# Operand sums of the 512-to-2048 weights on GpSimd, and three pairs of the last matrix formed early, kept in DRAM and read back

## The chip, the cores and the metric

The kernel runs on one core of one Trainium2 chip. The metric is device time in microseconds of one execution. An execution is called a run; the time before is the median of three runs.

## The reference, cut to what matters

```
out_g, out_l = attention with 32 global positions and a band of +-32 around each local one
x = concat([out_g, out_l]) as (2176, 512)
h = max(x @ w1, x @ w2, x @ w3)          # 512 -> 768
y = h @ w_out                            # 768 -> 512
g = softplus(y @ w_in)                   # 512 -> 2048
return g @ w2_out                        # 2048 -> 512
```

All arrays come in as float64. The kernel takes the words apart itself and computes with float32 halves: an operand is a high part plus a low part, and a product is three matmuls (high by high, high by low, low by high).

## The kernel before, in words

There are four stages. The first is the attention. The second, 512 to 768 to 512, works on eight units of tokens, 0 to 7 (256 tokens where the number is even, 288 where it is odd); `up` multiplies a unit by one of the three up weights (12 matmuls, 18 `up`s for a unit), `down` and `down_all` multiply by `w_out`. The third, 512 to 2048, and the fourth, 2048 to 512, use Strassen's scheme: seven products of half-size blocks in place of eight, so that operands are first summed and differenced. The names PE, DVE, ACT, POOL and SP stand for TensorE, VectorE, ScalarE, GpSimd and the queue that issues the DMAs. The order on every engine is the order in which the code is written out; generators (`d4`, `d5`, `vgen`, `vloads`, `words`, `load_x`, `load_o`) are advanced a step at a time between pieces of the main work, at rates such as `WU`, `WD`, `VD`, `VL`, `VE`.

Names that the steps need:

- `split(w, src)` makes the two halves of an operand: ACT copies the high part (L644), POOL subtracts it from the source (L645).
- `dec_w4` forms the seven operands of one of eight pairs of blocks of `w_in`: it reads a pair `qi` from DRAM, sums it (L671, L672, L678, L686, four instructions of 256 columns) and splits it. Pairs 0 to 3 (`d4`) are formed beside units 6 and 7, pairs 4 to 7 (`d5`) beside the first half of the third stage.
- `load_o(t)` does the same to the tokens of one quarter: sums on DVE (L709, L712, L717, L725, 544 columns each), seven splits on ACT and POOL. It runs one quarter ahead of the products that use it; its split of `x[1]` is the first that `prods_b` of the next quarter reads.
- The third stage is 32 steps i. In step i, PE does `prods_a(i)` (3 products, 18 matmuls of 272 columns), `prods_c(i-1)` (2), `prods_b(i)` (2). ACT copies the first product to `e` (L964), DVE adds it to the second (L965), and only then may `prods_b` add on to that second product: its matmuls at L943 wait for L965. DVE's L973, L974, L986 and L987 form the other sums.
- `make_v` (the generator `vgen`) forms the operands of the last matrix, eight pairs p: it reads `vq`, sums it (L1020 with 512 columns, L1022, L1023, L1025 with 256) and splits it. It starts at step 16; pairs 4 and 5 go to a place that is free from step 28, pairs 6 and 7 are formed beside the first products of the fourth stage.
- The fourth stage is a list of items (block of tokens, pair). For each item DVE does three sums (L1085 to L1087) and two low parts (L1093), ACT two high parts (L1092), PE 21 matmuls of 256 columns (L1097 to L1099).
- `load_x(u)` reads a unit's tokens `xr` from DRAM, ACT and DVE split them (L113, L114). The tokens of units 6 and 7 are both loaded at the end of unit 5, one behind the other.
- All DMAs are issued by SP, in order: an issue that waits holds back those behind it.
- Pools that matter: `wp`, 24 buffers for weights and operands, `cp`, 8 more from unit 6 on, and `raw`, 3 buffers. `room` and `free4` count how many `w_in` operands may be placed.

Of the kernel before, what the change touches and what calls it, by code (L numbers as in the profile page):

```python
# [8 lines left out]
F32 = mybir.dt.float32  # L9
# [3 lines left out]
ALU = mybir.AluOpType  # L13
# [8 lines left out]
def body(ctx, tc, kq, vw, vb, qg, w1, w2, w3, w_out, w2_in, w2_out, out):  # L22
# [475 lines left out]
    od = [dram.tile([128, 4, 544], F32, name=f"od{i}") for i in range(4)]  # L498
    gd = [dram.tile([128, 4, 2176], F32, name=f"gd{i}") for i in range(4)]
# [69 lines left out]
    def down_all(u):  # L569
# [3 lines left out]
        for f in range(6):  # L573
            w = W[3, f]
# [72 lines left out]
    n4, free4 = [0], [0]  # L647

# [7 lines left out]
    def dec_w4(ps, tile_q):  # L656
        half = None
# [9 lines left out]
        for p in ps:  # L667
# [3 lines left out]
            nc.vector.tensor_tensor(s[:, 0], a21, a22, op=ALU.add)  # L671
            nc.vector.tensor_tensor(s[:, 1], s[:, 0], a11, op=ALU.subtract)  # L672
# [26 lines left out]
            wi[p] = [wa[:, 0], wa[:, 1], h, wb[:, 0], wb[:, 1], wc[:, 1], wc[:, 0]]  # L699

# [32 lines left out]
    with tc.manual_schedule():  # L733
# [116 lines left out]
        for u in range(6):  # L850
# [4 lines left out]
            loads_x = [] if u == 0 else [6, 7] if u == 5 else [u + 1]  # L855
# [32 lines left out]
        d4 = dec_w4(range(4), lambda: dp.tile([128, 4, 256], F32, tag="raw", name="qi", bufs=3))  # L888
# [292 lines left out]
        for i in range(32):  # L1181
# [29 lines left out]
        vgate[0] = 2  # L1211
# [82 lines left out]
```

## Time and profile before

| | us |
|---|---|
| median of 3 runs | 808.92 (807.06 to 809.92) |
| the profiled execution | 808.67 |
| its span, first to last instruction | 807.0 |
| PE busy | 761.6 (94%) |
| DVE busy | 601.6 (75%) |
| ACT busy | 362.3 (45%) |
| POOL busy | 231.4 (29%) |
| granted TensorE clock, mean | 0.989 of 2.4 GHz |

The profiled execution lies 1.7 us above its span. A busy time is a sum over instructions that are queued one behind the other; PE's matmuls overlap, so PE can be busy all the time and still be slow, which the count of matmuls in a stretch shows better. The third stage runs from 433.7 to 617.7 us, the fourth from there to the end; units 6 and 7 are PE's work from 356.4 to 433.7 us.

### The profile page before, as it was taken

The page shows a single profiled execution, that of the slowest core. Times are in us where ns is not written, and L with a number is a line of the kernel's source. Part 1 is how long each engine was busy: PE and PEld are TensorE (multiplying, and loading weights), DVE is VectorE, ACT ScalarE, POOL GpSimd, SP SyncE. Part 2 cuts the span into 40 slices and gives each one's busy share as a digit, 9 for nine tenths or more (in the row PEclk, how much of TensorE's full clock was granted, in tenths as well). Part 3 has the DMA queues.
Part 4 walks back from the last instruction along what each step waited for, and adds up shares of the span by engine and source line. Part 5 has one row for each costly group of instructions (what it writes and reads, how often), then busy time and mean ns, then how long its engine had stood idle before and what let it go on. Part 6 is the DMA issues. An engine that isn't in the chain of part 4 may idle for free.

```text
span 807.0 us, 18054 instructions
## 1 busy us (share of the span) xinstructions
PE 761.6 (94%) x6984; PEld 728.7 (90%) x6984; DVE 601.6 (75%) x1486; ACT 362.3 (45%) x935; POOL 231.4 (29%) x212
## 2 busy tenths in 40 slices
PE   5789998999999999999999989999988889999998
PEld 3579997999989889999999989999888789999998
DVE  5978965988976967328922778557767989999996
ACT  6865446545544523024312445435435444444443
POOL 4545431222111200006800766315654330000000
PEclk9999999999999999999999999999999999999999
DMA  8858028777776636123003544345536803444432
GB/s 334 341 185 299 37 90 275 231 268 253 260 263 215 202 124 208 28 74 132 15 1 124 192 137 144 120 164 181 189 123 214 262 2 105 131 132 132 131 93 79
DMA packets 76134, 130.94 MB, mean 162 GB/s; under 512 B 9616, under 2 KB 45328, under 8 KB 76048
## 3 DMA queue, kind: packets, MB, share of 16 engines
q1 hardware_dynamic: 76048, 129.79, 47.5%
q8 instruction: 55, 0.90, 0.5%
q14 instruction: 31, 0.25, 0.1%
HBM read 91.29 MB, written 38.47 MB: 161 GB/s over the span
## 4 chain that ended last, share of the span: by engine, by line
PE 76%; DVE 12%; issue 3%; ACT 3%; DMA 3%; POOL 2%; SPq 0%; POOLq 0%; ACTq 0%; DVEq 0%
PE pu L513 8%; PE pu L514 8%; PE pu L515 8%; PE z L1098 6%; PE z L1099 6%; PE z L1097 6%; PE z L943 6%; PE z L945 6%; PE z L944 6%; PE pd L560 2%; PE pd L561 2%; PE pd L559 2%; DMA raw<-in_w_dram 2%; PE pog L294 2%; PE ps L142 2%
## 5 line engine op out<-in xcount | busy, mean ns | idle before, releaser
L513 PE MATMUL pu<-xh,w 128*128 128x256 f32 (+1 forms) x576 | 169.4, 294 | 1.5 <-ACT xo L255 1.0
L515 PE MATMUL pu<-xh,w 128*128 128x256 f32 (+1 forms) x576 | 166.9, 290 | 0.8 <-POOL w L451 0.8
L514 PE MATMUL pu<-xl,w 128*128 128x256 f32 (+1 forms) x576 | 167.4, 291 | 0.2
L943 PE MATMUL z<-o,wi 128*128 128x272 f32 x448 | 131.7, 294 | 11.4 <-DVE h L965 10.1
L1099 PE MATMUL z<-v,oo 128*128 128x256 f32 x480 | 137.1, 286 | 4.0 <-DVE oo L1093 4.0
L1098 PE MATMUL z<-v,oo 128*128 128x256 f32 x480 | 136.7, 285 | 1.3 <-POOL v L645 1.3
L1097 PE MATMUL z<-v,oo 128*128 128x256 f32 x480 | 135.9, 283 | 1.7 <-ACT oo L1092 0.9
L945 PE MATMUL z<-o,wi 128*128 128x272 f32 x448 | 131.3, 293 | 0.0
L944 PE MATMUL z<-o,wi 128*128 128x272 f32 x448 | 130.7, 292 | 0.0
L513 PEld LDWEIGHTS pu<-xh,w 128*128 128x128 f32 x576 | 109.3, 190 | 4.8 <-ACT xo L255 1.2
L515 PEld LDWEIGHTS pu<-xh,w 128*128 128x128 f32 x576 | 109.0, 189 | 1.2 <-POOL w L451 1.2
L514 PEld LDWEIGHTS pu<-xl,w 128*128 128x128 f32 x576 | 109.2, 190 | 0.8 <-DVE xl L114 0.6
L943 PEld LDWEIGHTS z<-o,wi 128*128 128x128 f32 x448 | 86.6, 193 | 13.1 <-DVE h L965 11.2
L1099 PEld LDWEIGHTS z<-v,oo 128*128 128x128 f32 x480 | 91.6, 191 | 5.6 <-DVE oo L1093 5.6
L1097 PEld LDWEIGHTS z<-v,oo 128*128 128x128 f32 x480 | 92.1, 192 | 2.5 <-ACT oo L1092 1.6
L1092 ACT ACTIVATE oo<-sm 128x640 fp32r<-128x640 f32 (+1 forms) x72 | 49.8, 692 | 98.2 <-DVE sm L1087 92.3
L1098 PEld LDWEIGHTS z<-v,oo 128*128 128x128 f32 x480 | 91.5, 191 | 1.7 <-POOL v L645 1.7
L945 PEld LDWEIGHTS z<-o,wi 128*128 128x128 f32 x448 | 86.4, 193 | 0.0
L944 PEld LDWEIGHTS z<-o,wi 128*128 128x128 f32 x448 | 86.3, 193 | 0.0
L164 POOL TENSOR_TENSOR s<-s,rs 128x512 f32<-128x512 f32 x32 | 36.2, 1132 | 157.7 <-DVE rs L162 85.5
L645 POOL TENSOR_TENSOR o<-ot,o 128x544 fp32r<-128x544 f32 x36 | 51.2, 1434 | 68.4 <-DVE h L986 38.9
L996 ACT ACTIVATE a<-h 128x816 f32<-128x816 f32 x32 | 28.4, 887 | 92.7 <-DVE h L974 92.7
(145 smaller groups left out, 1665.1 us busy)
## 6 DMA issues: line engine op xcount, KB each, us to landing
gd<-a SPq DMA_DIRECT2D x32, 544.0 KB, 3.1
gl<-gd SPq DMA_DIRECT2D x32, 512.0 KB, 5.6
kq<-in_kq_dram SPq DMA_DIRECT2D x31, 448.0 KB, 5.6
raw<-in_w_out_dram SPq DMA_DIRECT2D x22, 512.0 KB, 4.6
raw<-in_w_dram SPq DMA_DIRECT2D x18, 512.0 KB, 7.9
vt<-in_vw_dram SPq DMA_DIRECT2D x16, 512.0 KB, 6.3
raw<-in_w_in_dram SPq DMA_DIRECT2D x16, 512.0 KB, 4.6
ot<-od SPq DMA_DIRECT2D x24, 272.0 KB, 3.7
```

Of the source, the lines that this page charges most:

```text
L164: nc.gpsimd.tensor_tensor(s[:, :, 0:128], s[:, :, 0:128], rs.unsqueeze(2).to_broadcast([128, 4, 128]), op=ALU.mult)
L513: nc.tensor.matmul(p, lhsT=w[:, 0, k], rhs=xh[:, k, 0:n], start=(k == 0), stop=False)
L514: nc.tensor.matmul(p, lhsT=w[:, 0, k], rhs=xl[:, k, 0:n], start=False, stop=False)
L515: nc.tensor.matmul(p, lhsT=w[:, 1, k], rhs=xh[:, k, 0:n], start=False, stop=(k == 3))
L645: nc.gpsimd.tensor_tensor(w[:, 1], src, w[:, 0].bitcast(F32), op=ALU.subtract)
L943: nc.tensor.matmul(z, lhsT=w[:, 0, k], rhs=x[:, 0, k], start=st and k == 0, stop=False, skip_group_check=True)
L944: nc.tensor.matmul(z, lhsT=w[:, 0, k], rhs=x[:, 1, k], start=False, stop=False, skip_group_check=True)
L945: nc.tensor.matmul(z, lhsT=w[:, 1, k], rhs=x[:, 0, k], start=False, stop=sp and k == 1, skip_group_check=True)
L1092: nc.scalar.activation(oh[:, a:b], src, AF.Copy)
L1097: nc.tensor.matmul(p, lhsT=oh[:, a], rhs=w[:, 0], start=st, stop=False, skip_group_check=True)
L1098: nc.tensor.matmul(p, lhsT=oh[:, a], rhs=w[:, 1], start=False, stop=False, skip_group_check=True)
L1099: nc.tensor.matmul(p, lhsT=ol[:, a], rhs=w[:, 0], start=False, stop=sp, skip_group_check=True)
```

## The change

- Unit 5's loop now loads unit 6's tokens between its own `up`s; only unit 7's remain for its end.
- `dec_w4` takes the engine of its sums as an argument: VectorE for pairs 0 to 3, as before, GpSimd for pairs 4 to 7.
- A new generator, `spill_v`, follows pairs 0 to 3 in `d4`, beside units 6 and 7: it forms pairs 5, 6 and 7 of the last matrix (sums on DVE, splits on ACT and POOL) and writes the halves to DRAM (`vd`). `WU` and `WD`, the steps of `d4` per `up` and per step of `down_all`, go from 0.9 and 1.0 to 1.1 and 1.2, and `d4` is now drained before the third stage.
- `make_v` forms only pairs 0 to 4. The sums of pairs 0 to 2 are on GpSimd, those of 3 and 4 on VectorE; each pair's sums are advanced in turns with the splits of the pair before. It starts at step 14 at a steady rate of 2.2 steps.
- `vload` reads pairs 5 to 7 back with four DMAs each, one DMA in each of the steps 29 to 31, one after them, and one for each of the first items.

```
+    vd = {p: dram.tile([128, 7, 2, 256], F32, name=f"vd{p}") for p in range(5, 8)}
...
-            nc.vector.tensor_tensor(s[:, 0], a21, a22, op=ALU.add)
-            nc.vector.tensor_tensor(s[:, 1], s[:, 0], a11, op=ALU.subtract)
+            eng.tensor_tensor(s[:, 0], a21, a22, op=ALU.add)
+            eng.tensor_tensor(s[:, 1], s[:, 0], a11, op=ALU.subtract)
...
+    def sum_v(eng, q, s):
+        eng.tensor_tensor(s[:, 0:2], q[:, 0:4:2], q[:, 1:4:2], op=ALU.add)
+        yield
+        eng.tensor_tensor(s[:, 2], q[:, 0], q[:, 3], op=ALU.add)
+        eng.tensor_tensor(s[:, 3], q[:, 1], q[:, 3], op=ALU.subtract)
+        yield
+        eng.tensor_tensor(q[:, 2], q[:, 2], q[:, 0], op=ALU.subtract)
+        yield
+
+    def spill_v(ps):
...
+        for p in ps:
+            q, s = [dp.tile([128, 4, 256], F32, tag="raw", name="qv", bufs=3) for _ in range(2)]
+            read_v(q, p)
...
+            for _ in sum_v(nc.vector, q, s):
+                yield
+            for n, y in enumerate((q[:, 0:4:3], s[:, 0:2], s[:, 2:4])):
...
+                w = w4tile()
+                split(w.rearrange("p a t n -> p t a n"), y)
+                write(vd[p][:, 2 * n:2 * n + 2], w)
+                yield
...
-        WU = 0.9
-        WD = 1.0
+        WU = 1.1
+        WD = 1.2
...
+                if u == 5 and i == 2:
+                    if f == 0:
+                        ensure(6)
+                        x6 = load_x(6)
+                    next(x6, None)
-            loads_x = [] if u == 0 else [6, 7] if u == 5 else [u + 1]
+            loads_x = [] if u == 0 else [7] if u == 5 else [u + 1]
...
+        d4 = itertools.chain(d4, spill_v(range(5, 8)))
...
-        d5 = dec_w4(range(4, 8), lambda: wp.tile([128, 4, 256], F32, tag="w", name="qi"))
-        need4(3)
+        d5 = dec_w4(range(4, 8), lambda: wp.tile([128, 4, 256], F32, tag="w", name="qi"), nc.gpsimd)
+        for _ in d4:
+            pass
...
+            for p in range(5):
+                while p == 4 and not vgate[0]:
                     yield
+                nx = iter(())
+                if p < 4:
+                    vs[p + 1] = wp.tile([128, 4, 256], F32, tag="w", name="vs")
+                    nx = sum_v(nc.vector if p > 1 else nc.gpsimd, vq[p + 1], vs[p + 1])
                 for _ in vsplit(p):
                     yield
+                    if next(nx, 1) is None:
+                        yield
...
+            if i > 28:
+                next(vloads)
```

Three places show what moves. The first is DVE in the third stage, step 5 to step 6 (`h`, `e` and `z` are the product sums, `ot` the tokens being summed, `qi` and `s` the `w_in` pair). Before:

```order
L987 TENSOR_TENSOR h<-h,z 128x272
L712 TENSOR_TENSOR ot<-ot 128x544
L671 TENSOR_TENSOR s<-qi 128x256
L672 TENSOR_TENSOR s<-s,qi 128x256
L678 TENSOR_TENSOR qi<-qi 128x256
L965 TENSOR_TENSOR h<-e,z 128x272
```

The same place on DVE now, where L762, L767, L1020, L1028, L1029 and L1042 are what L712, L717, L965, L973, L974 and L987 were:

```order
L1042 TENSOR_TENSOR h<-h,z 128x272
L762 TENSOR_TENSOR ot<-ot 128x544
L1020 TENSOR_TENSOR h<-e,z 128x272
L1028 TENSOR_TENSOR h<-e,z 128x272
L1029 TENSOR_TENSOR h<-h,z 128x272
L767 TENSOR_TENSOR ot<-ot,t_6547 128x544
```

The three sums of `qi` and `s` that stood between the two sums of `h` are gone from DVE.

The second is POOL over steps 5 to 7, where the tokens of quarter 2 (`o_6472` before, `o_6543` now) and a `w_in` pair are split in turns. Before:

```order
L645 TENSOR_TENSOR o_6472<-ot,o_6472 128x544
L645 TENSOR_TENSOR o_6472<-t_6476,o_6472 128x544
L645 TENSOR_TENSOR o_6472<-ot,o_6472 128x544
L645 TENSOR_TENSOR wi<-qi,wi 128x2x256
L645 TENSOR_TENSOR wi<-qi,wi 128x256
L645 TENSOR_TENSOR o_6472<-ot,o_6472 128x544 x2
L645 TENSOR_TENSOR wi<-s,wi 128x2x256
L645 TENSOR_TENSOR o_6472<-ot,o_6472 128x544 x2
```

The same place on POOL now:

```order
L647 TENSOR_TENSOR o_6543<-ot,o_6543 128x544
L647 TENSOR_TENSOR o_6543<-t_6547,o_6543 128x544
L647 TENSOR_TENSOR o_6543<-ot,o_6543 128x544
L673 TENSOR_TENSOR s<-qi 128x256
L674 TENSOR_TENSOR s<-s,qi 128x256
L647 TENSOR_TENSOR wi<-qi,wi 128x2x256
L680 TENSOR_TENSOR qi<-qi 128x256
L647 TENSOR_TENSOR wi<-qi,wi 128x256
L647 TENSOR_TENSOR o_6543<-ot,o_6543 128x544 x2
L688 TENSOR_TENSOR qi<-qi,s 128x256
L647 TENSOR_TENSOR wi<-s,wi 128x2x256
L647 TENSOR_TENSOR o_6543<-ot,o_6543 128x544 x2
```

Four sums of 256 columns now stand ahead of the last two splits of the quarter's tokens, which are `x[1]` and `x[6]`.

The third is DVE beside units 6 and 7, from the last sum of pair 3 on (`m` is the running maximum over the three up products `pu`, `hh` and `hl` its halves). Before:

```order
L686 TENSOR_TENSOR qi<-qi,s 128x256
L527 TENSOR_TENSOR m<-m,pu 128x256 x2
L544 CAST hh<-m 128x256
L545 TENSOR_TENSOR hl<-m,hh 128x256
L527 TENSOR_TENSOR m<-m,pu 128x288 x2
L527 TENSOR_TENSOR m<-m,pu 128x256
```

The same place on DVE now:

```order
L688 TENSOR_TENSOR qi<-qi,s 128x256
L528 TENSOR_TENSOR m<-m,pu 128x288
L767 TENSOR_TENSOR ot<-ot,t_5349 128x544
L528 TENSOR_TENSOR m<-m,pu 128x288
L528 TENSOR_TENSOR m<-m,pu 128x256
L707 TENSOR_TENSOR qv<-qv 128x512
L709 TENSOR_TENSOR qv<-qv 128x256
L710 TENSOR_TENSOR qv<-qv 128x256
L528 TENSOR_TENSOR m<-m,pu 128x256
L545 CAST hh<-m 128x256
L546 TENSOR_TENSOR hl<-m,hh 128x256
L712 TENSOR_TENSOR qv<-qv 128x256
```

The last sum of pair 3 comes three `up`s earlier, and the four sums of each spilled pair (L707, L709, L710, L712) follow between the maxima.

## Rows read from the trace of the kernel before

**Rows 1.** Busy time by stretch: start:end, us, each engine's busy us (instructions), PEclk, DMA share, GB/s.

```profile
361.00:367.40 6.40, 5.88 (x25) 5.04 (x26) 3.40 (x8) 3.50 (x7) 0.00 (x0) 0.74 0.95 303
433.70:498.00 64.30, 58.74 (x451) 58.08 (x452) 46.01 (x74) 29.10 (x59) 37.55 (x28) 0.97 0.47 158
498.00:560.00 62.00, 62.00 (x497) 62.00 (x497) 39.45 (x76) 27.85 (x56) 23.04 (x19) 1.00 0.45 161
560.00:621.70 61.70, 56.28 (x421) 55.50 (x420) 44.24 (x79) 29.91 (x60) 35.96 (x28) 0.94 0.52 177
621.70:667.00 45.30, 38.33 (x280) 35.49 (x279) 40.96 (x84) 20.21 (x40) 17.27 (x11) 0.96 0.39 125
667.00:803.00 136.00, 136.00 (x1138) 136.00 (x1137) 124.61 (x327) 60.15 (x125) 0.00 (x0) 1.00 0.36 115
```

**Rows 2.** PE's waits from 355 us: line, released by: us in total, times, longest.

```profile
PE z L943 <- DVE h L965: 10.1, 5, 2.8
PE z L1099 <- DVE oo L1093: 4.0, 8, 2.0
```

**Rows 3.** Timeline of DVE, steps 5 and 6: start us, us, engine, line, operation.

```profile
466.55 1.65 DVE L712 TENSOR_TENSOR ot<-ot 128x544 f32<-128x544 f32 x1
468.12 1.58 DVE L671 TENSOR_TENSOR s<-qi 128x256 f32<-128x256 f32 x1
469.73 1.45 DVE L672 TENSOR_TENSOR s<-s,qi 128x256 f32<-128x256 f32 x1
471.11 1.48 DVE L678 TENSOR_TENSOR qi<-qi 128x256 f32<-128x256 f32 x1
472.51 0.42 DVE L965 TENSOR_TENSOR h<-e,z 128x272 f32<-128x272 f32 x1
```

**Rows 4.** Timeline of DVE, sums of the last matrix with POOL idle.

```profile
612.25 0.68 DVE L1020 TENSOR_TENSOR vs<-vq 128x512 f32<-128x512 f32 x1
612.85 0.42 DVE L1022 TENSOR_TENSOR vs<-vq 128x256 f32<-128x256 f32 x1
```

**Rows 5.** Timeline of DVE, the same sums beside POOL's work, step 23.

```profile
562.32 0.98 DVE L1020 TENSOR_TENSOR vs<-vq 128x512 f32<-128x512 f32 x1
563.22 0.95 DVE L1022 TENSOR_TENSOR vs<-vq 128x256 f32<-128x256 f32 x1
564.10 1.58 DVE L1023 TENSOR_TENSOR vs<-vq 128x256 f32<-128x256 f32 x1
565.60 1.55 DVE L1025 TENSOR_TENSOR vq<-vq 128x256 f32<-128x256 f32 x1
```

**Rows 6.** POOL by line and shape, 510 to 550 us: busy us, mean ns, idle before.

```profile
L645 POOL TENSOR_TENSOR v<-vs,v 128x512 fp32r<-128x512 f32 x2 | 2.5, 1294 | 4.0 <-PE z L945 4.0
L645 POOL TENSOR_TENSOR v<-vq,v 128x256 fp32r<-128x256 f32 x1 | 0.7, 742 | 2.5 <-ACT v L644 2.5
```

**Rows 7.** Timeline of POOL, steps 6 and 7, in brackets the idle time before.

```profile
475.17 2.85 POOL L645 TENSOR_TENSOR o<-ot,o 128x544 fp32r<-128x544 f32 x2 [2.00 <-ACT o L644]
481.30 2.69 POOL L645 TENSOR_TENSOR o<-ot,o 128x544 fp32r<-128x544 f32 x2 [2.02 <-ACT o L644]
```

**Rows 8.** Timeline of PE, the first matmul of `prods_b(8)`.

```profile
484.35 0.29 PE L943 MATMUL z<-o,wi 128*128 128x272 f32 x1
```

**Rows 9.** Busy time by stretch, beside units 6 and 7; columns as in rows 1.

```profile
368.00:403.00 35.00, 35.00 (x281) 35.00 (x280) 32.87 (x44) 14.79 (x31) 29.23 (x22) 1.00 0.11 38
403.00:434.00 31.00, 30.09 (x237) 29.63 (x236) 6.14 (x14) 6.35 (x17) 1.36 (x1) 1.00 0.07 23
```

**Rows 10.** Timeline of DVE and of PE at the start of the fourth stage.

```profile
622.16 1.88 DVE L1093 TENSOR_TENSOR oo<-sm,oo 128x640 fp32r<-128x640 f32 x1
...
624.10 0.39 PE L1099 MATMUL z<-v,oo 128*128 128x256 f32 x1 [1.97 <-DVE oo L1093]
```

**Rows 11.** Timeline of PE, the first matmul of unit 7.

```profile
361.25 0.40 PE L513 MATMUL pu<-xh,w 128*128 128x288 f32 x1 [0.44 <-ACT xh L113]
```

**Rows 12.** DMA issues: out<-in, queue, operation, count, KB each, median us to landing.

```profile
gl<-gd SPq DMA_DIRECT2D x32, 512.0 KB, 5.6
```

More of the change, by code (lines that the diff above doesn't have):

```diff
@@ L573, in down_all @@
         for f in range(6):
+            need((3, f))
             w = W[3, f]
@@ L647, in body @@
     n4, free4 = [0], [0]
+    halves = {}
     def w4tile():
@@ L654, in room, with dec_w4 @@
         return n4[0] + n <= NC + free4[0]
-    def dec_w4(ps, tile_q):
-        half = None
+    def dec_w4(ps, tile_q, eng):
         qs = {}
@@ L699, in dec_w4, with read_v, write @@
             wi[p] = [wa[:, 0], wa[:, 1], h, wb[:, 0], wb[:, 1], wc[:, 1], wc[:, 0]]
+    def read_v(q, p):
+        nc.sync.dma_start(out=q.rearrange("p a n -> p (a n)"), in_=qd["v"][p].rearrange("p a n -> p (a n)"))
+    def sum_v(eng, q, s):
[7 more added lines that the diff above has]
+    def spill_v(ps):
+        half, out = None, []
+        def write(d, w):
+            out.append((d, w))
+            if len(out) > 1:
+                x = out.pop(0)
+                nc.sync.dma_start(out=x[0], in_=x[1].bitcast(F32))
+                if x[1].shape[1] == 2 and len(x[1].shape) == 4:
+                    free4[0] += 1
+        for p in ps:
[6 more added lines that the diff above has]
+            for n, y in enumerate((q[:, 0:4:3], s[:, 0:2], s[:, 2:4])):
+                while not room(1):
+                    yield
+                w = w4tile()
+                split(w.rearrange("p a t n -> p t a n"), y)
+                write(vd[p][:, 2 * n:2 * n + 2], w)
+                yield
+            if p % 2 == 0 or half is None:
+                while not room(1):
+                    yield
+                half = w4tile()
+            split(half[:, p % 2], q[:, 2])
+            write(vd[p][:, 6], half[:, p % 2])
+            yield
+        for d, w in out:
+            nc.sync.dma_start(out=d, in_=w.bitcast(F32))
+        yield
     def load_o(t, pool, temp):
@@ L1031, in vsplit @@
                 vs["o"] = op0.tile([128, 2, 7, 2, 256], F32R, tag="o", name="v45", bufs=1)
-            if p in (4, 5):
-                v = [vs["o"][:, p - 4, i] for i in range(7)]
-                both = [vs["o"][:, p - 4, i:i + 2] for i in (0, 2, 4)]
+                v = [vs["o"][:, 0, i] for i in range(7)]
+                both = [vs["o"][:, 0, i:i + 2] for i in (0, 2, 4)]
             else:
@@ L1210, in body @@
                 prep(i - 30)
-        vgate[0] = 2
+        for _ in vgen:
+            pass
+        next(vloads)
         mults(*items[0])
@@ L1224, in body @@
             start(i + LG - 1 + SA)
-            while x[1] not in V:
-                next(vgen, None)
-            vdebt[0] += VE
-            while vdebt[0] >= 1:
-                vdebt[0] -= 1
-                next(vgen, None)
+            next(vloads, None)
             if i > 0:
```

68 lines of the change are left out of this document (36 added, 32 removed).

## The prediction, made before the changed kernel was run

> **What bounds the kernel now.** I first read PE's busy time by stretch, because PE is busy 94% of the span and only a count of matmuls tells where it is slow. In the third stage's middle (498 to 560 us) PE starts 497 matmuls in 62.0 us, one every 0.1247 us, at full granted clock and without a wait; in the fourth stage from 667 us on, 1138 in 136 us, one every 0.1195 us [rows 1]. No engine holds PE up there, so these are the paces that nothing here can beat. At them, the other stretches lose: 433.7 to 498 us, 64.3 - 451 x 0.1247 = 8.1 us; 560 to 621.7 us (400 matmuls of the third stage, 21 of the fourth), 61.7 - 49.9 - 2.5 = 9.3 us; 621.7 to 667 us, 45.3 - 280 x 0.1195 = 11.8 us; 361 to 367.4 us, 25 matmuls of 288 columns at 0.1247 x 288/272 = 0.132 us each, 6.4 - 3.3 = 3.1 us [rows 1]. That is 32.3 us, and it is all that this change can win.
>
> Then I read who is waited for. In the third stage PE waits five times, 10.1 us, for DVE's L965, and in the fourth eight times, 4.0 us, for DVE's low parts L1093 [rows 2]. The rest of the 32.3 us is the slower clock behind the longer waits: it is granted 0.97, 0.94 and 0.96 of full speed in those stretches, 0.74 in 361 to 367.4 us [rows 1]; the engine had just waited each time.
>
> Last, why DVE is late. In step 5 to 6 four sums stand ahead of L965: 1.65, 1.58, 1.45 and 1.48 us, 6.2 us in all [rows 3]. A sum of 256 columns takes 0.42 us with POOL idle, one of 512 columns 0.68 us [rows 4]; beside POOL's work the same lines take 0.95 to 1.58 us [rows 5]. L965 itself, which reads one operand from PSUM, keeps its 0.42 us right behind them [rows 3]. So a DVE sum with both operands in SBUF costs up to one of POOL's instructions more than its own time, and a row of such sums makes L965 late.
>
> How late is too late: from the end of the product that L965 reads, PE still has zc (6 matmuls), two products of `prods_c` (12) and one of `prods_b` (6), 24 x 0.1247 = 3.0 us. L965 takes 0.4, so DVE may run some 2.5 us behind. One contended sum ahead of L965 is hidden, four are not.
>
> **Third stage, steps 0 to 15 (8.1 us lost).** The 16 sums of `d5` leave DVE. What is left between two sums of `h` is one sum of tokens, at most 1.65 us [rows 3], under the 2.5. So the three waits of this stretch go. What is next late: POOL. It gets 16 sums more. Its subtraction takes 1.29 us for 512 columns and 0.74 for 256 [rows 6], so a moved sum costs about 0.74. The tightest place is the split of `x[1]`: at step 7 POOL starts it at 481.30, after 2.02 us of idling, and is done half of 2.69 us later, at 482.65; PE wants it at 484.35, 1.7 us on [rows 7, 8]. Between step 5 and there it idled 2.00 + 2.02 us [rows 7], but some 3.1 us of these steps are PE's own loss, which goes (the 2.8 us wait of rows 2 and some clock), so about 0.9 us of idling stay, and 2.6 us can be taken in. The change puts four sums ahead, 3.0 us. So PE waits about 0.4 us there, perhaps 1.5 if DVE's three token sums hold POOL up once more. In the other quarters three or fewer sums are extra. I leave 2.5 us lost here: 1 for POOL, 0.8 for the stage's start, which nothing touches, and 0.7 for what I don't see. Bounds: 1 to 6. Gain 5.6.
>
> The skill speaks against this move (GPSIMD Engine Reference, "4.1 Engine selection"): sums of two operands belong on VectorE, about twice as fast. Alone the rows agree, 0.42 against 0.74 us. By that rule alone the move would cost 16 x 0.32 = 5 us where the sums are on PE's path, and the sum would come out at 795 with the gain of these steps gone too; beside POOL's work the rows have 1.48 us where the rule has VectorE's lone 0.42, so I don't follow it.
>
> **Third stage, steps 16 to 31 (9.3 us).** Sums of the last matrix for pairs 0 to 2 go to POOL; DVE keeps those of pairs 3 and 4, and they come in turns with splits. In the order, one place is left with three of them ahead of L965, after step 23, and one with two. Before, step 23 had all four, 0.98 + 0.95 + 1.58 + 1.55 = 5.1 us [rows 5], and PE waited 1.9 us; without the last 1.55 some 0.4 us stay. With the ACT burst at the stage's end I leave 1.5 lost (bounds 0.7 to 4). Gain 7.8.
>
> **Fourth stage, start (11.8 us).** DVE is over its limit: 40.96 us busy for 280/21 = 13.3 items, 3.07 us an item where PE needs 21 x 0.1195 = 2.51 [rows 1]. Later it needs 124.61/54.2 = 2.30 with POOL idle [rows 1]. The change takes out two pairs' sums and all 17.27 us of POOL's work [rows 1], and with POOL's work the stretching: one L1093 took 1.88 us there, and PE waited 1.97 us for it [rows 10]. DVE then keeps up. It still starts with little lead: I leave 2.5 lost. In its place come 12 DMAs, 5.5 MB, less 1.6 MB of pair reads that go: 3.9 MB over some 45 us is 87 GB/s beside 125 to 177 GB/s at a DMA share of 0.39 to 0.52 [rows 1], so a share below 0.8. SP issues them between the reads of `gl`, which take 5.6 us to land [rows 12] and are issued two or three pairs of items (5 us each) ahead. That hides a read that is some 4 us slower, not one that is 10 us slower. Pairs 5, 6 and 7 are wanted at items 7, 9 and 11, 17 to 28 us after the first item, and the last DMA is issued at item 7; a landing of up to 10 us is hidden. Bounds 1 to 7. Gain 9.3.
>
> **Unit 7's tokens (3.1 us).** Its first matmul waited for ACT's copy of tokens that had been read last [rows 11]; now only they are read at the end of unit 5, where unit 6's stood, which came in time. I leave 0.3. The DMAs, copies and subtractions for unit 6 move into unit 5's loop, eight instructions of 0.4 us beside PE. Gain 2.8.
>
> **Units 6 and 7: the price.** PE loses nothing here now, but DVE is busy 32.87 of 35 us, POOL 29.23, and both are almost idle afterwards: 6.14 and 1.36 of 31 us [rows 9]. The change adds three pairs: on DVE 0.68 + 3 x 0.42 = 1.9 us each alone [rows 4], 5.1 beside POOL [rows 5], 5.8 to 15 us in all; on POOL 3 x (3 x 1.29 + 0.74) = 13.8 us [rows 6]. The idle time after 403 us, 25 us on DVE and 30 on POOL, holds both. But the sums of pairs 0 to 3 now come 22% faster, three `up`s earlier. PE's cover is PSUM: a maximum may be some five `up`s late, 5 x 12 x 0.125 = 7.5 us. By my count of the contended times DVE is up to 7 us late around the end of pair 3 and at the first spilled pair. And behind the last spilled sum on ACT stand the copies that free PSUM for `down_all(7)`. Bounds: 0 (all hidden) to 8 (a few us of waiting and the slower clock behind it); I take 1.2, nearer to zero, as no row shows PE waiting for a maximum. Draining `d4` ahead of the third stage costs nothing if DVE is done by then, for which the idle 25 us leave room.
>
> **The sum**, against the profiled execution: 808.67 - (5.6 + 7.8 + 9.3 + 2.8) + 1.2 = 784.4. The profiled run lies 0.25 us under the median of the runs, so about 784.5 us is forecast.
>
> **Rivals.**
> 1. DVE and POOL are overfull beside units 6 and 7. In favour: a DVE sum waits for POOL's instruction, so that the times of the two add up: POOL 29.23 + 1.36 [rows 9] and 13.8 for the spilled pairs, 44; DVE's sums and low parts, 9 + 16 + 12 of 256 columns and 3 + 4 longer ones at about 0.42 and 0.7 [rows 4], 20. That is 64 of 66 us. Against: part of POOL's 30.6 us is already such waiting. It costs 4 to 8 us more than forecast: 788 to 793. The Trainium skill (SBUF — State Buffer, "Who interferes with whom") has it that a VectorE instruction with two SBUF inputs and a GpSimd instruction that reads SBUF exclude each other for the whole instruction, which is what makes this rival; rows 3 to 5 agree.
> 2. The reads in the fourth stage collide: `gl` lands late, DVE waits, half of the gain there goes, with the clock: 789 to 792.
> 3. POOL is late for `x[1]` in three quarters, 2 us each and the clock, against rows 7 and 8 in one quarter only: 787 to 791.
> 4. Nothing takes the lost time's place: 808.7 - 32.3 + 1.8 (the stage's start and the end) = 778.
> 5. Slower: the maxima late in every one of the twelve groups of `up`s. It takes DVE sums that all wait out a whole POOL instruction: 28 sums at 1.5 us and 4 of tokens at 1.65 [rows 3], 48.6 us; 22 maxima at L965's 0.42, 9.2; five pairs of halves at 1.9, 9.6; together 67 us where PE needs 33 `up`s x 12 x 0.129 = 51: 16 us lost, and at half clock behind each wait another 10. With rival 3 on top, 811 to 814. It decides from a lateness of 7.5 us on; against it, PE was not held up there once before.
> 6. The change doesn't do what it says: the stalls come from the token sums, not the moved ones, and stay. Then 16 us of the gain are gone: 800 or so. Rows 3 speak against it: of 6.2 us, 4.5 are the moved ones.
>
> **How the numbers follow.** Forecast (781 to 788) 0.53; rival 1 0.14; rival 2 0.10; rival 3 0.08; rival 4 0.07; rival 6 and mixtures above 793, 0.04 (a quarter of it within 0.3%); rival 5 or something unseen that costs as much, 0.04 (a quarter of it within 0.3%). The range takes in the forecast, rivals 1 to 3 and the upper half of rival 4: 778 to 793. A measurement of this kernel can tell 0.3%, 2.4 us. Faster by more than that: 0.92 + 0.03 = 0.95; within it 0.02; slower 0.03.
>
> **What would show it.** PE's waits for L965's successor (L1020) fall from 10.1 us to under 2; the granted clock is 1.00 over both halves of the third stage. Waits of PE for POOL's splits of `o` at L998 would mean rival 3; waits at the maxima or at `down_all` in units 6 and 7, rival 1; waits for the low parts behind a DMA of `gl`, or for `v` behind a DMA of `vd`, rival 2. The first matmul of unit 7 follows unit 6's without a gap. I am wrong if units 6 and 7 lose more than 5 us, or if the fourth stage loses more than 6.

## The result, and the profile after

The changed kernel takes 786.66 us (median of 4 runs, 784.15 to 790.38), the kernel before 809.42 in the same session: a ratio of 0.973, 95% interval 0.968 to 0.977. 784.5 was forecast, with a range of 778 to 793. A second set of runs gave 787.53 us and a ratio of 0.973 (0.971 to 0.975).

The profiled run is the longest of the first four, 790.38 us with a span of 788.7. Its busy time by stretch, columns as in rows 1: the third stage's two ends and middle, the fourth stage's start and its rest.

```profile
434.70:498.00 63.30, 61.87 (x490) 61.42 (x491) 37.75 (x67) 32.82 (x65) 48.20 (x41) 1.00 0.53 174
498.00:560.00 62.00, 61.85 (x495) 61.62 (x493) 30.71 (x63) 28.05 (x56) 37.60 (x36) 1.00 0.43 155
560.00:613.40 53.40, 49.98 (x386) 49.32 (x385) 38.16 (x68) 25.23 (x50) 31.45 (x24) 0.97 0.63 210
613.40:667.00 53.60, 53.11 (x437) 52.42 (x436) 46.39 (x119) 24.31 (x48) 0.00 (x0) 1.00 0.60 205
```

At the paces of rows 1 these lose 63.3 - 490 x 0.1247 = 2.2 us, 53.4 - 365 x 0.1247 - 21 x 0.1195 = 5.4 (21 of its matmuls are the fourth stage's), and 53.6 - 437 x 0.1195 = 1.4, where the kernel before lost 8.1, 9.3 and 11.8 [rows 1]. In the fourth stage DVE now needs 46.39 us for 437 / 21 = 20.8 items, 2.23 us an item, under the 2.51 that PE needs; it was 3.07.

PE's waits of the changed kernel from 340 us on: line, released by: us, times, longest.

```profile
PE z L998 <- ACT e L1019: 2.1, 1, 2.1
PE z L999 <- POOL o L647: 1.6, 3, 0.9
PE z L998 <- DVE h L1020: 1.2, 1, 1.2
PE z L998 <- ACT o L586: 0.5, 1, 0.5
PE pd L580 <- ACT o L586: 0.4, 1, 0.4
PE z L1166 <- DVE oo L1160: 0.4, 1, 0.4
PE pu L514 <- DVE m L528: 0.3, 1, 0.3
```

L998, L1019, L1020 and L1160 are L943, L964, L965 and L1093 of before. The wait for DVE's `h` has gone from 10.1 us to 1.2, that for the low parts from 4.0 to 0.4 [rows 2]. For ACT's copy L1019 PE now waits 2.1 us in step 28; before it waited 0.8 us, in step 31. POOL's subtraction of tokens L647 is a new row, and a small one for the maxima L528. The two for ACT's L586 (L584 before) were there as they are. The wait for unit 7's tokens [rows 11] has gone.

To compare runs I took, for every pair of neighbouring matmuls, the gap between their starts less the pace of rows 1, and summed it by stage (us, from 330 us on). It counts waits and slow clock alike; "Units 6, 7" is the last 60 us ahead of the third stage's first product, which is in it.

| kernel | unit 7's start | units 6, 7 | steps 0-15 | steps 16-31 | fourth stage | sum |
|---|---|---|---|---|---|---|
| before | 3.8 | 1.3 | 7.9 | 9.3 | 12.4 | 34.8 |
| changed | 0.3 | 2.1 | 2.6 | 5.4 | 2.4 | 12.8 |
| changed, second trace | 0.3 | 2.3 | 2.6 | 3.9 | 2.6 | 11.7 |
| sums_on_dve | 0.3 | 3.0 | 7.9 | 5.4 | 2.4 | 19.0 |
| v_sums_on_dve | 0.3 | 2.5 | 2.5 | 7.7 | 2.5 | 15.5 |
| x6_late | 2.7 | 4.4 | 2.5 | 3.9 | 2.5 | 16.1 |
| no_spill | 0.3 | 1.9 | 2.6 | 8.7 | 13.0 | 26.5 |
| before_sums | 2.5 | 1.4 | 2.5 | 7.8 | 12.3 | 26.5 |
| pool_fill | 0.3 | 2.3 | 0.1 | -0.2 | 2.5 | 5.0 |
| vd_21 | 0.3 | 2.1 | 2.5 | 4.7 | 2.6 | 12.3 |
| own22 | 0.3 | 2.2 | 2.5 | 1.7 | 2.4 | 9.2 |
| own_early | 0.3 | 2.7 | 1.8 | 1.6 | 2.5 | 9.0 |
| best250 | 0.3 | 2.1 | 0.1 | 1.0 | 2.5 | 6.0 |
| old_pace | 0.3 | 2.5 | 2.5 | 5.4 | 2.4 | 13.2 |

The two profiled times differ by 808.67 - 790.38 = 18.3 us, the table's sums by 22.0. The rest, 3.7 us, lies ahead of 330 us: unit 5's first matmul, ahead of which nothing in the program is changed, starts at 321.72 us in place of 318.01. The first 150 us, same columns: in the changed kernel's first trace the granted clock was 0.97,

```profile
0.00:150.00 150.00, 129.46 (x1394) 115.32 (x1395) 113.14 (x348) 85.86 (x268) 59.53 (x74) 0.97 0.61 218
```

in its second trace 0.99,

```profile
0.00:150.00 150.00, 129.57 (x1430) 115.08 (x1430) 115.84 (x355) 89.03 (x279) 59.57 (x74) 0.99 0.61 221
```

and in the kernel before 1.00:

```profile
0.00:150.00 150.00, 129.79 (x1448) 115.11 (x1450) 116.28 (x355) 89.28 (x280) 59.25 (x74) 1.00 0.62 223
```

In the second trace the first product of the third stage starts at 431.97 us, in the first at 434.67. So the first trace was an unlucky run by 2.7 us there, and the 790 of its profile is not what the kernel takes.

### The profile page after: what moved, and what is told of

Same layout as the page of the kernel before. It is cut to its first block, busy times and chain, and to the rows that moved or that the text cites. A ratio compares the mean times of both kernels' runs of the same rounds, so it can differ in the third digit from the quotient of the medians.

```text
span 788.7 us, 18081 instructions
## 1 busy us (share of the span) xinstructions
PE 755.8 (96%) x6984; PEld 726.0 (92%) x6984; DVE 580.5 (74%) x1458; ACT 363.2 (46%) x935; POOL 250.6 (32%) x240
## 4 chain that ended last, share of the span: by engine, by line
PE 71%; DVE 8%; POOL 7%; DMA 6%; issue 4%; ACT 3%; SPq 1%; POOLq 0%; ACTq 0%; DVEq 0%
PE pu L514 7%; PE z L1166 7%; PE pu L516 6%; PE z L1165 6%; PE z L1164 6%; PE pu L515 6%; PE z L998 5%; PE z L999 5%; PE z L1000 5%; POOL o L647 3%; DMA raw<-in_w_dram 2%; POOL wi L647 2%; PE pd L561 2%; PE pd L560 2%; PE pd L562 2%
## 5 line engine op out<-in xcount | busy, mean ns | idle before, releaser
L998 PE MATMUL z<-o,wi 128*128 128x272 f32 x448 | 129.9, 290 | 3.8 <-ACT e L1019 2.1
L999 PE MATMUL z<-o,wi 128*128 128x272 f32 x448 | 130.1, 290 | 1.7 <-POOL o L647 1.6
L1000 PE MATMUL z<-o,wi 128*128 128x272 f32 x448 | 129.8, 290 | 0.0
L998 PEld LDWEIGHTS z<-o,wi 128*128 128x128 f32 x448 | 85.4, 191 | 4.5 <-ACT e L1019 2.3
L999 PEld LDWEIGHTS z<-o,wi 128*128 128x128 f32 x448 | 85.0, 190 | 2.6 <-POOL o L647 2.5
L1000 PEld LDWEIGHTS z<-o,wi 128*128 128x128 f32 x448 | 85.1, 190 | 0.0
L1160 DVE TENSOR_TENSOR oo<-sm,oo 128x640 fp32r<-128x640 f32 (+1 forms) x72 | 55.0, 764 | 16.4 <-ACT oo L1159 12.6
L528 DVE TENSOR_TENSOR m<-m,pu 128x256 f32<-128x256 f32 (+1 forms) x96 | 41.3, 432 | 32.7 <-PE pu L516 26.4
```

The lines of the kernel that those rows point to most:

```text
L528: nc.vector.tensor_tensor(m, m, p, op=ALU.max)
L998: nc.tensor.matmul(z, lhsT=w[:, 0, k], rhs=x[:, 0, k], start=st and k == 0, stop=False, skip_group_check=True)
L999: nc.tensor.matmul(z, lhsT=w[:, 0, k], rhs=x[:, 1, k], start=False, stop=False, skip_group_check=True)
L1000: nc.tensor.matmul(z, lhsT=w[:, 1, k], rhs=x[:, 0, k], start=False, stop=sp and k == 1, skip_group_check=True)
L1160: nc.vector.tensor_tensor(ol[:, a:b], src, oh[:, a:b].bitcast(F32), op=ALU.subtract)
```

## The experiments: each part undone

**The sums of the weights, back on VectorE.**

```
-        d5 = dec_w4(range(4, 8), ..., nc.gpsimd)
+        d5 = dec_w4(range(4, 8), ..., nc.vector)
```

> One part undone: the 16 sums of the weights for pairs 4 to 7 of the 512-to-2048 stage go back from GpSimd to VectorE; all else as in the changed kernel. Theory (they are what made L1020 late, because beside POOL's work each takes about 1.5 us): in steps 0 to 15 PE waits again for L1020, 5 to 7 us in three waits, with a granted clock under 1.00 behind the longest, and the three waits for POOL's subtraction of o (1.6 us together in the changed kernel) go, as POOL has 16 sums less. Time 4 to 8 us longer: 791 to 795 us. Rival (the waits came from the token sums, which stay on DVE in both): PE's waits for L1020 stay under 2 us, and the time is 785 to 787.

Measured: 794.34 us, ratio to before 0.983 (0.980 to 0.986). Its waits of PE for `h`:

```profile
PE z L998 <- DVE h L1020: 6.7, 4, 2.7
```

Three of the four are in steps 0 to 15 (1.35, 2.73, 1.36 us), and no row for POOL's L647 is left. Steps 0 to 15 lose 7.9 us, as before the change, against 2.6. The theory holds; the rival, that the token sums alone made the waits, falls.

**The same part alone, put into the kernel before.**

```
-    def dec_w4(ps, tile_q):
+    def dec_w4(ps, tile_q, eng):
...
-            nc.vector.tensor_tensor(s[:, 0], a21, a22, op=ALU.add)
+            eng.tensor_tensor(s[:, 0], a21, a22, op=ALU.add)
...
+        d5 = dec_w4(range(4, 8), ..., nc.gpsimd)
```

> The kernel before with one part of the change alone: the 16 sums of the weights for pairs 4 to 7 on GpSimd. Theory: the three waits for L965 in steps 0 to 15 go, POOL's late x[1] costs some 2 us in their place, and the rest stays: 7.8 us lost between 440 and 500 us become about 2.3, 5 to 6 us less than the kernel before. Rival (the parts need each other: the sums only pay where DVE is freed elsewhere too): 0 to 3 us less.

Measured: 802.70 us against 809.31, ratio 0.993 (0.991 to 0.995), 6.6 us less. Steps 0 to 15 lose 2.5 us, and 1.4 us of waits for POOL stand there. The part pays by itself.

**Why a sum is slow on VectorE: POOL reads nothing.**

```
-        nc.gpsimd.tensor_tensor(w[:, 1], src, w[:, 0].bitcast(F32), op=ALU.subtract)
+        if staged[0]:
+            nc.gpsimd.tensor_tensor(w[:, 1], src, w[:, 0].bitcast(F32), op=ALU.subtract)
+        else:
+            nc.gpsimd.memset(w[:, 1].bitcast(F32), 0.0)
...
+        d5 = dec_w4(range(4, 8), ..., nc.vector)
```

> The sums of pairs 4 to 7 are on VectorE, as in the run with that part undone, and in the last two stages POOL writes a constant where it forms low parts, so that its instructions read nothing from SBUF; the low parts of those weights and tokens are left out, and all else is issued as it was. Theory (a sum waits out a POOL instruction that reads SBUF, and that made the row of sums late): the sums take 0.42 and 0.68 us throughout, and PE's three waits for L1020 in steps 0 to 15 (1.35, 2.73 and 1.36 us in that run) go; under 1 us is lost between 440 and 500 us, against 7.8. Rival (four sums ahead of L1020 are too many whatever POOL does): those waits stay above 1 us each.

Measured: 780.17 us in one run; nothing is lost in the third stage. The same four sums by line and shape from 434 to 500 us (count, busy us, mean ns, idle before), in the run with the sums on VectorE beside POOL's subtractions:

```profile
L673 DVE TENSOR_TENSOR s<-qi 128x256 f32<-128x256 f32 x3 | 4.6, 1549 | 0.0
L688 DVE TENSOR_TENSOR qi<-qi,s 128x256 f32<-128x256 f32 x3 | 4.4, 1459 | 0.0
L680 DVE TENSOR_TENSOR qi<-qi 128x256 f32<-128x256 f32 x3 | 3.5, 1158 | 0.0
L674 DVE TENSOR_TENSOR s<-s,qi 128x256 f32<-128x256 f32 x3 | 3.3, 1106 | 0.1
```

and in this run, where the lines are three numbers higher:

```profile
L676 DVE TENSOR_TENSOR s<-qi 128x256 f32<-128x256 f32 x4 | 1.7, 418 | 0.0
L677 DVE TENSOR_TENSOR s<-s,qi 128x256 f32<-128x256 f32 x4 | 1.7, 425 | 0.1
L683 DVE TENSOR_TENSOR qi<-qi 128x256 f32<-128x256 f32 x3 | 1.3, 418 | 0.0
L691 DVE TENSOR_TENSOR qi<-qi,s 128x256 f32<-128x256 f32 x3 | 1.3, 418 | 0.0
```

1.1 to 1.5 us became 0.42. A fill is also shorter than a subtraction, so the sums meet POOL less often; but where they do meet it they keep their time. Timeline of POOL in this run, a pair of fills, and of DVE:

```profile
479.27 1.04 POOL L650 MEMSET o<- 128x544 f32 x2
...
479.73 0.43 DVE L677 TENSOR_TENSOR s<-s,qi 128x256 f32<-128x256 f32 x1
```

Of DVE's 44 sums in the third stage eight overlap a fill, all at 0.42 or 0.72 us, what they take alone (0.72 for the 544 columns of tokens). It is POOL's reading that stretches them, not four sums as such. The Trainium skill (SBUF — State Buffer, "Who interferes with whom") has the same: a VectorE instruction with two SBUF inputs contends with a GpSimd instruction that reads SBUF, not with one that only writes it. The two runs agree with both halves.

**The early sums of the last matrix, back on VectorE.**

```
-            for _ in sum_v(nc.gpsimd, vq[0], vs[0]):
+            for _ in sum_v(nc.vector, vq[0], vs[0]):
...
-                    nx = sum_v(nc.vector if p > 1 else nc.gpsimd, vq[p + 1], vs[p + 1])
+                    nx = sum_v(nc.vector, vq[p + 1], vs[p + 1])
```

> One part undone: the sums of pairs 0 to 2 of the last matrix go back to VectorE; their order and pace stay as in the changed kernel. Theory (row of contended sums ahead of L1020): one or two waits for L1020 of 1 to 2 us each in steps 15 to 23, 1 to 5 us with the clock, 788 to 792 us. Rival (spreading the sums over more steps was what counted, and the engine doesn't matter): no new wait, POOL has more room, 785 to 787 us.

Measured: 790.58 us, ratio 0.977 (0.973 to 0.981). No new wait came: the one after step 23 grew from 1.2 to 2.2 us, the granted clock behind it fell to 0.83 for ten us (1.00 in both traces of the changed kernel), and steps 16 to 31 lose 2.3 us more than in the changed kernel's first trace. But the row of three sums there didn't get longer (4.2 us from its start to the next sum of `h`, 4.6 in the changed kernel). It began later, behind a read. Timeline of DVE in this run:

```profile
564.83 1.35 DVE L707 TENSOR_TENSOR vs<-vq 128x512 f32<-128x512 f32 x1 [1.05 <-DMA vq<-qv]
```

So the extra wait is not shown to be VectorE's slower sums; what made that read late is not tested. In time the part is worth 3 to 4 us by the medians, and the two intervals overlap. That spreading the sums did most of the work in these steps is argued only, since no run spreads them and does nothing else: waits for `h` are 4.6 us before, 2.2 with the sums spread on VectorE, 1.2 with three pairs on GpSimd.

**Unit 6's tokens late again.**

```
-                if u == 5 and i == 2:
...
-                    next(x6, None)
-            loads_x = [] if u == 0 else [7] if u == 5 else [u + 1]
+            loads_x = [] if u == 0 else [6, 7] if u == 5 else [u + 1]
```

> One part undone: the tokens of unit 6 are read again at the end of unit 5, with those of unit 7. Theory: the first matmul of unit 7 waits for ACT's copy of its tokens (2.7 us in the kernel before) and runs at a slower clock for a while, 3 us: 789 to 790 us, all of it between 350 and 370 us. Rival (what is won there is lost again in units 6 and 7, whose sums now come sooner): 786 to 787 us.

Measured: 792.67 us, ratio 0.980 (0.977 to 0.984). Between 360 and 370 us 2.5 us are lost, as expected; 2.2 us more than in the changed kernel are lost from 390 to 410 us, where two maxima L528 are 1.0 and 1.3 us late. So the part is worth about 4.7 us, more than the 2.8 forecast for it, and the time lies above the 789 to 790 expected. Right ahead of the two late maxima stand sums of pair 3 (L673 and L674, 1.50 and 1.45 us; L680 and L688, 1.51 and 1.59). Why they come late here is not tested.

**Nothing kept in DRAM: pairs 5 to 7 formed late.**

```
-        d4 = itertools.chain(d4, spill_v(range(5, 8)))
...
+            for p in range(5, 8):
+                while p > 5 and vgate[0] < 2:
+                    yield
...
+                for _ in sum_v(nc.vector, vq[p], vs[p]):
+                    yield
...
+            while x[1] not in V:
+                next(vgen, None)
```

> One part undone: pairs 5 to 7 of the last matrix are formed by DVE, ACT and POOL from step 28 on and in the fourth stage, as in the kernel before, and nothing is kept in DRAM or read back; the early sums of pairs 0 to 4, the sums on GpSimd and unit 6's tokens stay as changed. Theory (these three pairs and POOL's work beside them are what made DVE late for the low parts): from 610 to 670 us 7 to 11 us are lost, against 1.4 in the changed kernel, PE waits several times for L1160's counterpart, and the 0.7 us of waits in units 6 and 7 go: 792 to 797 us. Rival (the earlier start of the last matrix was enough, because fewer pairs are left): 787 to 790 us.

Measured: 802.72 us, ratio 0.992 (0.990 to 0.995), worse than I expected. The fourth stage loses 13.0 us, 10.4 to 10.6 more than with the spill; PE waits there six times for DVE's low parts (2.2 us) and twice for ACT's high parts (2.6), which stand behind DVE's sums. The other 5 were not in the forecast: this kernel runs 3.5 turns a step from step 28 on, as the kernel before did (a turn is one advance of the generator), and PE waited 2.4 us in step 31 for ACT's copy to `e` (L1018 in this kernel) and was granted 0.83 over the ten us behind it. Of the whole gain the spill is the largest part: 10.4 of 22 us by the table.

## The experiments: what the forecast had missed

**The wait for L1019.** Timelines of ACT, of POOL and of PE in the changed kernel, around step 28 (start us, us, ..., in brackets the idle time before and what ended it):

```profile
585.54 0.66 ACT L646 ACTIVATE o<-ot 128x544 fp32r<-128x544 f32 x1
589.68 0.63 ACT L646 ACTIVATE v<-vs 128x512 fp32r<-128x512 f32 x1 [3.47 <-POOL o L647]
590.21 0.38 ACT L1019 ACTIVATE e<-z 128x272 f32<-128x272 f32 x1
...
586.62 3.02 POOL L647 TENSOR_TENSOR o<-ot,o 128x544 fp32r<-128x544 f32 x2
...
590.64 0.60 PE L998 MATMUL z<-o,wi 128*128 128x272 f32 x1 [2.10 <-ACT e L1019]
```

ACT's copy of pair 3's third part stands 3.47 us and starts 0.04 us after POOL's two subtractions of tokens end (589.64). It doesn't read those tokens: it writes the buffer in which they lie. By the program the ring `w` of 24 buffers is full here, and the next one to come free is that of the tokens POOL reads last. L1019 stands behind the copy on ACT, and PE behind L1019. The first try was to move the copies a little.

```
-        VD = 2.2
+        VD = 2.1
```

> One number of the changed kernel is changed: 2.1 turns of the last matrix's generator a step in place of 2.2. The third split of pair 3 then goes to a buffer whose last reader on POOL was queued 12 ACT instructions earlier, where in the changed kernel it goes to the buffer of the tokens that POOL is to read last, one ACT instruction earlier. Theory (ACT stood 3.5 us at that copy, with L1019 behind it, and PE waited 2.1 us for L1019 and then ran at 0.83): the wait at step 28 goes, with the slow clock behind it, 3 to 3.5 us: 783 to 784 us. Rival (POOL is simply behind there, and something else waits for it a step later): one wait of 1 to 2 us for POOL or ACT in steps 27 to 31 stays, 785 to 787 us.

Measured: 787.92 us, ratio 0.976 (0.971 to 0.980): no gain. The wait is gone, and another stands in its place. Timeline of DVE:

```profile
582.00 0.69 DVE L707 TENSOR_TENSOR vs<-vq 128x512 f32<-128x512 f32 x1 [4.81 <-DMA vq<-qv]
582.61 0.43 DVE L1020 TENSOR_TENSOR h<-e,z 128x272 f32<-128x272 f32 x1
```

At 2.1 turns a step the read of pair 4 and its first sum fall into one step, so the sum, and L1020 behind it, wait for the DMA; PE waited 2.3 us, and 1.4 us for ACT later. The rival held. Next the buffer itself: late tokens go to the scratch buffer of the weights' sums.

```
-            s = sp.tile([128, 2, 256], F32, tag="s", name="s", bufs=1)
+            s = sp.tile([128, 2, 272], F32, tag="s", name="s", bufs=1)[:, :, 0:256]
...
+            if i == 0 and step_now[0] > 16:
+                return sp.tile([128, 2, 272], F32, tag="s", name="ot", bufs=1)
             if i == 0:
                 return wp.tile([128, 2, 272], F32, tag="w", name="ot")
```

> The changed kernel, in which one buffer of the weights' ring is set free: in the last two quarters the tokens that POOL reads last lie in the scratch buffer of the sums, which is idle by then. Pace and order stay. Theory (ACT's copy of pair 3 stood 3.5 us for that buffer, and the run with 2.1 turns a step only moved the shortage, to a pair read too shortly ahead of its sum): the wait for L1019 at step 28 goes with the 0.83 clock behind it, nothing takes its place, 3 to 3.5 us less than the changed kernel on this chip: 782 to 784 us. Rival (POOL's backlog is what counts): PE waits 1 us or more for something else between 580 and 610 us, and the time is that of the changed kernel within 1.5 us.

Measured: 785.80 us, ratio 0.971 (0.968 to 0.973); the changed kernel on the same chip took 787.53:

> The changed kernel itself, as the measure for the other three on the same chip. 784 to 788 us; PE's waits from 340 us on as in its first trace: 2.1 us for L1019, 1.6 us for POOL's subtraction of o, 1.2 us for L1020, under 0.5 us each for the rest; what differs between its runs is granted clock in the first 300 us.

Steps 16 to 31 lose 1.7 us, and nothing new appears: the wait was for the buffer. In time that is 1.7 us by the medians, with intervals that overlap, and less than the 3 to 3.5 expected. The likely reason is that the slow clock behind that wait is not in every run: the second trace had the same wait (1.98 us) without it.

**POOL late for the tokens.** Timelines of POOL and of PE in the changed kernel, steps 7 and 8:

```profile
474.65 2.66 POOL L647 TENSOR_TENSOR o<-ot,o 128x544 fp32r<-128x544 f32 x2
477.26 1.24 POOL L688 TENSOR_TENSOR qi<-qi,s 128x256 f32<-128x256 f32 x1
478.46 1.30 POOL L647 TENSOR_TENSOR wi<-s,wi 128x512 fp32r<-128x512 f32 x1
479.72 2.66 POOL L647 TENSOR_TENSOR o<-ot,o 128x544 fp32r<-128x544 f32 x2
...
477.37 0.39 PE L999 MATMUL z<-o,wi 128*128 128x272 f32 x1 [0.93 <-POOL o L647]
481.12 0.39 PE L999 MATMUL z<-o,wi 128*128 128x272 f32 x1 [0.50 <-POOL o L647]
```

The first wait is for x[4], the second for x[1], and a third of 0.15 us at 499.5 is for x[4] of the next quarter. POOL works from 465.6 to 486 us with no gap that the trace marks; the 2 us of idling that it had in rows 7 are used up. A quarter's first step leaves it idle, so, on top of the freed buffer:

```
-            for _ in range(1 + (k == 1)):
+            for _ in range(1 + (k == 0)):
```

> As the run before, and the extra turn of the weights' generator in each quarter of the 512-to-2048 stage comes at its first step, where POOL had idled 2 to 3 us, in place of its second. Theory (POOL is late for x[1] because its queue is full only in steps 2 to 4 of a quarter): the three waits for POOL's subtraction of o, 1.6 us in the changed kernel, fall to 0.5 or less, with the slower clock behind them 1.5 to 2 us more are won: 780.5 to 782.5 us. Rival (the earlier sums hold up DVE's token sums or ACT's copies in the first step): a new wait for ACT or DVE in steps 4 to 13, no gain.

Measured: 783.74 us, ratio 0.969 (0.965 to 0.972), above the 780.5 to 782.5 expected. The three waits are gone, and one new wait of 1.5 us came, at 465.75: ACT stood 3.3 us at a pair whose read had been issued a turn ahead (ACT's timeline, L1023 is the L1019 of this kernel).

```profile
464.78 0.63 ACT L646 ACTIVATE wi<-qi 128x512 fp32r<-128x512 f32 x1 [3.28 <-DMA qi<-qi]
465.31 0.38 ACT L1023 ACTIVATE e<-z 128x272 f32<-128x272 f32 x1
```

So the new wait took back most of what the three had cost: from 330 us on this trace loses 9.0 us, the run before 9.2. The 2.1 us between the medians of the two are not shown to come from the edit.

**All of it, with that read a turn earlier and the three sums of step 23 apart.**

```
             split(wb.rearrange("p a t n -> p t a n"), s)
+            if eng is nc.gpsimd and p < ps[-1]:
+                read(p + 1)
             yield
...
         eng.tensor_tensor(s[:, 2], q[:, 0], q[:, 3], op=ALU.add)
+        if not staged[0]:
+            yield
         eng.tensor_tensor(s[:, 3], q[:, 1], q[:, 3], op=ALU.subtract)
...
+        VD = 2.5
```

> The kernel with the freed buffer and the extra turn at the first step of a quarter, and two more moves: on GpSimd's pairs the next pair's read is issued a turn earlier (the 1.5 us wait for L1019's counterpart at 466 us stood behind ACT's copy of a pair that landed 3.3 us late), and the second and third sum of a pair of the last matrix are taken in two turns, at 2.5 turns a step in place of 2.2 (the three sums in a row of step 23 cost 1.4 us of waiting and 0.4 of clock). Theory: both waits go or fall under 0.4 us, some 3 us less: 779 to 782 us, 7 us or less lost from 330 us on, against 11.7 in the changed kernel. Rival (each wait that goes uncovers another one): something of 1 us or more appears in its place and the time stays at 783 to 785.

Measured: 782.07 us, ratio 0.967 (0.965 to 0.969), below the changed kernel's second interval, which starts at 0.971; its first, wider one starts at 0.968. Steps 0 to 15 lose 0.1 us. Its waits from 340 us on that reach 0.5 us:

```profile
PE z L1007 <- POOL o L647: 0.7, 1, 0.7
PE z L1006 <- ACT o L586: 0.5, 1, 0.5
```

**The pace beside units 6 and 7.**

```
-        WU = 1.1
-        WD = 1.2
+        WU = 0.9
+        WD = 1.0
```

> The changed kernel with the pace of the kernel before beside units 6 and 7 (0.9 and 1.0 turns in place of 1.1 and 1.2): the sums of pairs 0 to 3 come as late as they did, some ten turns of the three spilled pairs are left at the end of unit 7, and the program issues them ahead of the 512-to-2048 stage. Theory (the faster pace costs units 6 and 7 some 0.8 us, because POOL's subtractions stretch the sums ahead of the maxima L528, and is cheaper than the alternative): the wait for L528 goes, and the first product of the next stage waits for ACT and POOL to form some two and a half pairs' parts, 4 to 8 us by POOL's 1.29 us each: 788 to 795 us. Rival (the third stage's first steps hide the rest, since only its first products need those engines): under 1 us of new waiting at 432 to 445 us, 785 to 787 us.

Measured: 786.40 us, ratio 0.971 (0.968 to 0.975): neither better nor worse, and my theory was wrong on both counts. The wait for L528 stayed (0.8 us), and the late parts were done by 431.6 us, while PE was still in `down_all(7)`, so the rival's time (785 to 787) came out. The faster pace alone doesn't make L528 late, then. Nor do the spilled pairs alone: without them the wait is 0.35 us, as in the changed kernel's first trace. In this run two sums of 1.52 and 1.47 us stand right ahead of it (L673, L674); the kernel before had the same two, as long, without a wait. Which of the moved pieces does it stays open.

## Why the prediction was right, and where it was off

- **Steps 0 to 15.** 2.5 us were to be left, 2.2 are by the same sum; the gain was 5.9 for 5.6. The mechanism holds on both sides, undone and alone. The successor was POOL, as said: 1.6 us in three waits where 1 was put down, two in the quarter named and a third, of 0.15 us, at the start of the next; its largest is for x[4], two subtractions ahead of the x[1] that I had picked.
- **Steps 16 to 31.** This is the term that was mis-sized: 1.5 us left, bounds 0.7 to 4, and 5.4 measured. Two causes. Step 23's three sums were priced by rows 5 (0.98, 0.95, 1.58), so that 0.4 us would stay. Timeline of DVE after the change, step 23:

```profile
563.04 1.67 DVE L707 TENSOR_TENSOR vs<-vq 128x512 f32<-128x512 f32 x1
564.64 1.58 DVE L709 TENSOR_TENSOR vs<-vq 128x256 f32<-128x256 f32 x1
566.14 1.56 DVE L710 TENSOR_TENSOR vs<-vq 128x256 f32<-128x256 f32 x1
567.63 0.42 DVE L1020 TENSOR_TENSOR h<-e,z 128x272 f32<-128x272 f32 x1
```

  With POOL fuller, each sum met a whole POOL instruction: 4.8 us for 3.5, 1.8 us lost. The other 3.8 us are the wait for a buffer and the clock behind it, which was in no step of the prediction: I costed who computes, and not where the results of pairs formed earlier would lie. The sign that I had named, a granted clock of 1.00 over both halves, held for the first half; the second had 0.97 in the first trace and 1.00 in the second.
- **Fourth stage.** 2.5 left forecast, 1.4 measured up to 667 us, and 0.5 more behind it than before (0.8 for 0.3 by the count of the table), which I had not foreseen. The gain of 10.4 us is of the size argued (9.3): DVE's need fell below PE's. But not all of the loss before was DVE and the clock, as I had put it. Two more of PE's waits in the kernel before:

```profile
PE z L1098 <- POOL v L645: 1.3, 2, 1.1
PE z L943 <- ACT e L964: 0.8, 1, 0.8
```

  With two rows for ACT in the fourth stage (0.9 us for high parts of the items, 0.7 for those of pair operands) 3.7 us of what the prediction gave to the clock were waits for POOL and ACT. None of the three in the fourth stage is left in the changed kernel. My bound on the DMAs was wrong, though it cost nothing. Stretches of the changed kernel, columns as in rows 1, and its reads:

```profile
620.00:630.00 10.00, 10.00 (x86) 10.00 (x85) 8.12 (x21) 4.18 (x8) 0.00 (x0) 1.00 1.05 386
630.00:640.00 10.00, 10.00 (x86) 10.00 (x86) 8.12 (x21) 4.19 (x8) 0.00 (x0) 1.00 0.98 326
```

from 600 to 660 us (operation, count, KB each, median us to landing):

```profile
gl<-gd SPq DMA_DIRECT2D x13, 512.0 KB, 6.8
v<-vd SPq DMA_DIRECT2D x7, 512.0 KB, 7.5
```

  I had spread 3.9 MB evenly and put the DMA share below 0.8; it was about 1.0 for 20 us. From 600 to 660 us the reads of `gl` landed in 6.8 us (5.6 before, rows 12), those of pairs in 7.5, still within the 10 us that are hidden. PE never waited for either.
- **Unit 7's tokens.** 0.3 left forecast; none of the 3.1 us was lost again.
- **Units 6 and 7.** Priced at 1.2 us, 0.8 measured. The place was one of those named, the end of pair 3: the sums L680 and L688 took 1.51 and 1.58 us ahead of L528, and PE waited 0.35 us. That these sums alone make L528 late is not shown (see the last experiment).
- **The sum.** The forecast has 8.0 us of these terms left; the trace has 2.2 + 5.4 + 1.9 + 0.8 = 10.3. That makes 784.4 + 2.3 = 786.7 for the profiled run; its 790.38 has the 3.7 us ahead of 330 us on top. The second trace lost 1.1 us less from 330 us on and took 786.37. That the total came so near is in part luck: the forecast left 3.9 us too little for steps 16 to 31 and 1.6 too much for the other terms together. Of the rivals, 3 came in small (1.6 us in one quarter and the next one's start, not 2 us in each of three quarters); 1, 2, 4, 5 and 6 did not.

## What to carry to other kernels

When a row of two-input sums on VectorE is slow beside GpSimd's subtractions, count a whole GpSimd instruction for each sum; moving the sums to GpSimd itself can win although each is slower there. When work is moved earlier, look not only for the engine's time but for the buffer: in a full ring a copy waits for the last reader of someone else's data, and everything behind it on its in-order engine waits too. Move a read with its first use, and keep a step between them.

## What the hardware showed that I had not expected

The clock's answer to a wait is not the same in every run. In its first trace the changed kernel had waited 2.10 us for L1019 and was granted 0.83 over the next ten us, part of it at 1.2 GHz and the rest at 2.4:

```profile
590.00:600.00 10.00, 9.36 (x63) 9.36 (x64) 4.98 (x11) 4.85 (x11) 3.38 (x4) 0.83 0.66 215
```

In its second trace it had waited 1.98 us at the same place and was granted 1.00:

```profile
587.00:597.00 10.00, 9.03 (x72) 9.03 (x73) 4.98 (x12) 5.70 (x12) 4.74 (x5) 1.00 0.64 205
```

63 matmuls in ten us against 72; steps 16 to 31 lose 5.4 us in the one and 3.9 in the other. The same wait stands in five more traces. The ten us counted as in the first row here have 0.83 after 1.98 us in `sums_on_dve`, `v_sums_on_dve`, `no_spill` and `old_pace`, and 1.00 after 2.10 us in `x6_late`. So it is one or the other, and the length of the wait doesn't tell which. A term of "the clock behind a wait" is worth 0 to 1.5 us here, for a wait of 2 us, and a gain of that size is read from several traces, not from one.
